# One decode-attention kernel, two attention blocks: each TensorE round takes its own group's PV, V of the last two groups in two parts, and wo of A with four heads side by side

## The chip, the cores and the metric

The kernel runs on one core of a Trainium2 chip. A core has five engines with instruction streams of their own: TensorE (PE in the profile, its weight loads PEld), VectorE (DVE), ScalarE (ACT), GpSimd (POOL) and SyncE (SP). Sixteen DMA engines move data from the chip's memory into the core's own memory (SBUF); TensorE writes its results into PSUM. The streams meet only at semaphores. The metric is the device time of one execution in microseconds; the kernel before has a median of 672.45 us over 3 runs (671.89 to 672.48).

## The reference

There are two independent attention blocks, A and B, of the same sizes. Each decodes one token: one query row, 32 heads of 128 numbers, and a cache of 8192 keys and values per head, all in bf16.

```python
# for A and for B; x: 1x512, k_cache and v_cache: 32 heads x 8192 x 128
q = x @ wq                                  # 512 x 4096, then 32 heads of 128
scores = einsum("hd,hkd->hk", q, k_cache) * 128 ** -0.5
p = softmax(scores)                         # over 8192 keys
o = einsum("hk,hkd->hd", p, v_cache)
y = o.reshape(1, 4096) @ wo                 # 4096 x 512
# the result is y of A and y of B side by side: 1 x 1024
```

Each cache is 64 MiB, and there are four of them. Each of the four weight matrices is 4 MiB.

## The kernel before

**Tiling.** Four heads make a group; there are N = 16 groups, eight of A and then eight of B. A group's K is 8 MiB: the 128 partitions hold 4 heads times 32 stretches of 256 keys, so that a partition has 256 keys (T) of 128 numbers. There are two K buffers (`kn`, used in turn) and one V buffer (`vn`). The query weights of A and B (`wq`) lie in the V buffer at the start, and the output weights (`wo`) in K buffer 0 at the end.

**One group.** VectorE multiplies K in place by the query in four quarters (`plan_mul`, L307). TensorE sums each quarter over the 128 numbers of a key in 16 matmuls against the identity into one of two PSUM halves (`scores`, L461), and VectorE adds up what is left (`plan_sr`, L312). The largest score of each head is found by VectorE and two small TensorE transposes (`plan_max`, L319 to L323, with L499 and L502 on TensorE). ScalarE then takes four exponentials, one per head, and their row sums (`plan_exp`, L335). For PV, TensorE makes one matmul of four columns for each of the 256 key positions, with a tile of V as the weights (L490), after one matmul that adds up the row sums (L483). VectorE divides by the sums (`plan_o`, L341 and L342).

**The order of TensorE's work** is written out in `pe_program`. A hardware loop of 17 rounds makes, in round r, the first three quarters of group r's scores, then PV of group r-1, then the fourth quarter of group r's scores and its maximum. The last round has no scores. In it stands, ahead of PV of group 15, a block (`prog[mid0:mid1]`) that moves the finished heads into another layout (`relayout`, L388 to L394), multiplies A's heads by A's wo (`mm_a`, L405: 32 matmuls of one output row, 512 columns each) and the first 16 heads of B by their part of B's wo (`mm_b`, L419). What is left of B's wo follows the loop.

**VectorE's order** for group n is: two quarters of the product, `plan_o` of group n-2, then products and sums in turn, and the maximum.

**The DMA queue.** All bulk loads are issued by SyncE in one order, each after the wait that frees its buffer:

```python
load_v(n, pv_done(n - 1) if n else q_done)   # V of group n: PV of group n-1 has read the buffer
load_k(n + 2)                                # K of group n+2: scores of group n are done
```

So the order in the queue is wq of A and B, K0, K1, V0, K2, V1, K3 and so on. After V14 come wo of A, the first part of B's wo (16 heads), V15 in two parts (192 and 64 of the 256 key positions, `VT = 192`, the second with a semaphore of its own, `s_v2`), and then the other parts of B's wo in shrinking pieces.

Of the kernel before, what the change touches and what calls it, by code (L numbers as in the profile page):

```python
# [8 lines left out]
BF16 = mybir.dt.bfloat16  # L9
F32 = mybir.dt.float32  # L10

P = 128
# [11 lines left out]
class _Plan:  # L24
# [6 lines left out]
    def wait(self, eng, mark):  # L31
        if mark is None:
            return
        ctr, val = mark
        if val <= 0 or self.waited.get((eng, ctr.name), 0) >= val:
            return
        self.waited[(eng, ctr.name)] = val
        self.prog[eng].append((None, ctr, val))

    def op(self, eng, fn, ctr=None, needs=(), inc=1):  # L40
        for m in needs:
            self.wait(eng, m)
        self.prog[eng].append((fn, ctr, inc))
        if ctr is None:
            return None
        ctr.n += inc
        return ctr, ctr.n
# [28 lines left out]
def bass_concat_heads__mha_block_cached__gqa_block_cached__decode_kernel(  # L76
# [19 lines left out]
    H, Sk, Dh = ks[0].shape[1:]  # L96
    D = xs[0].shape[2]
    NOUT = wos[0].shape[1]
# [4 lines left out]
    G = 4  # L103
    HP = P // G
    T = Sk // HP
    assert T == 256
    GA = H // G
    N = NA * GA
    NB = 4
    HT = T // NB  # L110
    DW = 512 // HT
    VT = 192
# [7 lines left out]
    with ExitStack() as st:  # L120
# [3 lines left out]
        def sb(name, shape, dt):  # L124
            return ec(nc.sbuf_tensor(name, shape, dt))

        kn = [sb("k%d" % i, [P, T, Dh], BF16) for i in range(2)]
        vn = sb("vn", [P, T, Dh], BF16)
# [5 lines left out]
        wo_buf = [kflat[0][:, a * H * NOUT:(a + 1) * H * NOUT] for a in range(NA)]  # L134
        wo_sb = [b.rearrange("p (j n) -> p j n", n=NOUT) for b in wo_buf]

        qbc = sb("qbc", [P, N, Dh], BF16)
        pt = sb("pt", [P, T, G], BF16)
        s_sb = sb("s_sb", [P, T], F32)
        xrow = sb("xrow", [1, NA, D], BF16)  # L140
        xb = sb("xb", [P, NA, C, HP], BF16)
        ones_bf = sb("ones_bf", [P, P], BF16)
        ones_f = sb("ones_f", [P, P], F32)
        ident = sb("ident", [P, P], BF16)
        ident_f = sb("ident_f", [P, P], F32)
        m1 = sb("m1", [P, 1], F32)
        gm = sb("gm", [1, G], F32)
        gmx = sb("gmx", [1, P], F32)
        negb = sb("negb", [P, N], F32)
        rsum = sb("rsum", [P, G], F32)  # L150
# [3 lines left out]
        o2 = sb("o2", [P, NA, H], BF16)  # L154
# [3 lines left out]
        out_a = sb("out_a", [1, NOUT], BF16)  # L158
# [6 lines left out]
        acc = ps("acc", [P, 512])  # L165
        mtp = ps("mtp", [P, 512])
        bmp = ps("bmp", [P, 512])
        misc = ps("misc", [P, 512])
        yps = [ps("yps%d" % i, [P, 512]) for i in range(2)]

        pl = _Plan()
        op, wait = pl.op, pl.wait
# [22 lines left out]
        def pv_done(n):  # L195
            return c_pv, n + 1
# [7 lines left out]
        def dma(eng, dst, src, c, needs=()):  # L204
            return op(eng, lambda e: e.dma_start(dst, src), c, needs, inc=16)  # L205


        def const(fn, needs=()):
            return op("POOL", fn, c_pool, needs)

        i_onesb = const(lambda e: e.memset(ones_bf[:], 1.0))
        i_onesf = const(lambda e: e.memset(ones_f[:], 1.0))
        i_ident = const(lambda e: e.affine_select(
            out=ident[:], in_=ones_bf[:], pattern=[[1, P]], compare_op=ALU.is_equal,
            fill=0.0, base=0, channel_multiplier=-1), [i_onesb])
# [18 lines left out]
        def load_v(n, need, t0=0, t1=T, c=None):  # L234
            a, i = divmod(n, GA)
            src = vs[a][0, G * i:G * (i + 1)].rearrange("h (p t) d -> (h p) (t d)", p=HP)
            v_in[n] = dma("SP", vflat[:, t0 * Dh:t1 * Dh], src[:, t0 * Dh:t1 * Dh], c or s_v, [need])
# [30 lines left out]
        q_done = None  # L268
# [36 lines left out]
        def plan_mul(n, h):  # L305
            k = kn[n % 2][:, h * HT:(h + 1) * HT, :]
            mul_done[n, h] = op("DVE", lambda e: e.tensor_tensor(  # L307
                k, k, qbc[:, n:n + 1, :].broadcast_to([P, HT, Dh]), ALU.mult),
                c_mul, [k_in[n], qbc_ready[n]])

        def plan_sr(n, h):
            sr_done[n, h] = op("DVE", lambda e: e.tensor_reduce(  # L312
                s_sb[:, h * HT:(h + 1) * HT],
                rps[:, h % 2, :].rearrange("p (t d) -> p t d", d=DW), AX.X, ALU.add),
                c_sr, [red_done(n, h), p_done.get(n - 1)])
# [23 lines left out]
        def plan_o(n):  # L339
            a, i = divmod(n, GA)  # L340
            m = op("DVE", lambda e: e.reciprocal(rinv[:, n, :], misc[:, 0:G]), c_dve, [sum_done(n)])  # L341
            o_done[n] = op("DVE", lambda e: e.tensor_tensor(  # L342
                oD[:, a, G * i:G * (i + 1)], acc[:, 0:G], rinv[:, n, :], ALU.mult),
                c_o, [pv_done(n), m])

        load_k(0)
        load_k(1)
        for n in range(N):
            if n < N - 1:
                load_v(n, pv_done(n - 1) if n else q_done)  # L350
                if n + 2 < N:
                    load_k(n + 2)
            plan_mul(n, 0)
            plan_mul(n, 1)
            if n >= 2:
                plan_o(n - 2)
            plan_sr(n, 0)
            plan_mul(n, 2)
            plan_sr(n, 1)
            plan_mul(n, 3)  # L360
            plan_sr(n, 2)
            plan_sr(n, 3)
            plan_max(n)
            plan_exp(n)

# [5 lines left out]
        load_v(N - 1, None, VT, T, s_v2)  # L371
        for g in range(NPRE, len(WOB)):
            load_wob(g)

        plan_o(N - 2)


        mid0 = len(pl.prog["PE"])
# [19 lines left out]
        for h0, n, rows in WOB:  # L398
            if rows:
                relayout(1, h0, n)  # L400

        def mm_a(e):
            r = None
            for j in range(H):
                r = e.matmul(yps[0][0:1, :], o2[:, 0, j:j + 1], wo_sb[0][:, j, :],  # L405
                             start=(j == 0), stop=(j == H - 1))
            return r
        m = op("PE", mm_a, c_pe, [o2_ready[0, 0], woa_in, y_free[0]])
        m = op("ACT", lambda e: e.copy(out_a[:], yps[0][0:1, :]), c_act, [m])
        done_a = dma("ACT", out[0][:, 0:NOUT], out_a[:], s_out[0], [m])  # L410

        def mm_b(g):
            h0, n, rows = WOB[g]
# [11 lines left out]

        for g in range(NPRE):
            mm_b(g)
        wait("PE", misc_free[0])
        mid1 = len(pl.prog["PE"])


# [13 lines left out]
        def pe_program(e):  # L445
            prog = pl.prog["PE"]
            _emit(e, prog[:mid0])
            w_mul = _Stepped(e, c_mul, 1, 1)
            w_sr = _Stepped(e, c_sr, SR0 - 1, 1)
            w_g = _Stepped(e, c_g, 1, 1)  # L450
            w_o = _Stepped(e, c_o, O0, 1)
            w_p = _Stepped(e, c_p, G, G)
            w_v = _Stepped(e, s_v, 16, 16)

            def scores(slot, hs):
                for h in hs:
                    w_mul.wait()
                    w_sr.wait()
                    r = None
                    for i in range(Dh // DW):  # L460
                        r = e.matmul(  # L461
                            rps[:, h % 2, :].rearrange("p (t d) -> p t d", d=DW), ident[:],
                            kn[slot][:, h * HT:(h + 1) * HT, i * DW:(i + 1) * DW],
                            start=(i == 0), stop=(i == Dh // DW - 1))
                    r.then_inc(c_red.sem, 1)
                    w_mul.grow()
                    w_sr.grow()

            def scores_of(r, hs):
                with e.If(r % 2 == 0):  # L470
                    scores(0, hs)
                with e.Else():
                    scores(1, hs)

            with e.Fori(0, N + 1) as r:
                with e.If(r < N):
                    scores_of(r, range(0, NB - 1))
                with e.If(r == N):
                    _emit(e, prog[mid0:mid1])
                with e.If(r > 0):  # L480
                    w_o.wait()
                    w_p.wait()
                    e.matmul(misc[:, 0:G], ones_f[:], rsum[:], start=True, stop=True).then_inc(c_sum.sem, 1)  # L483
                    w_v.wait()
                    m = None
                    for t in range(T):
                        if t == VT:
                            with e.If(r == N):
                                e.wait_ge(s_v2.sem, 16)
                        m = e.matmul(acc[:, 0:G], vn[:, t, :], pt[:, t, :],  # L490
                                     start=(t == 0), stop=(t == T - 1))
                    m.then_inc(c_pv.sem, 1)
                    w_o.grow()
                    w_p.grow()
                    w_v.grow()
                with e.If(r < N):
                    scores_of(r, range(NB - 1, NB))
                    w_g.wait()
                    e.matmul(mtp[0:1, 0:P], m1[:], ident_f[:], start=True, stop=True).then_inc(c_gx.sem, 1)  # L499
                    w_g.grow()  # L500
                    w_g.wait()
                    e.matmul(bmp[:, 0:1], gmx[:], ones_f[0:1, 0:1], start=True, stop=True).then_inc(c_bc.sem, 1)  # L502
                    w_g.grow()
            _emit(e, prog[mid1:])

        for name, at in (("SP", block.sync), ("PE", block.tensor), ("ACT", block.scalar),
# [35 lines left out]
```

## Time and profile before

| | |
|---|---|
| median of 3 runs | 672.45 us (671.89 to 672.48) |
| the profiled execution: its time, its span | 671.92 us, 670.2 us |
| bytes read from memory | 285.21 MB |
| PE matmul busy | 439.5 us, 66% |
| VectorE busy | 342.6 us, 51% |
| ScalarE busy | 62.2 us, 9% |
| mean granted TensorE clock | 0.757 |

Everything below refers to the profiled execution, with times in microseconds from the start of its span. The page of the profile gives each engine's busy time, and the span in 40 slices with the busy share of the DMA engines and what they moved. A view of stretches gives the same for any piece of the span: after its limits and length come the busy time of PE, PEld, VectorE, ScalarE and GpSimd (with the number of instructions in brackets), the granted TensorE clock, the busy share of the DMA engines, and GB/s. A DMA packet is counted in the stretch in which it starts. The timeline has a line for each run of alike instructions: start, length, engine, line, operation, what it writes and reads, how many, and in brackets how long the engine was idle before it and what ended that. The list of DMA issues gives the time from issue to landing.

### The profile page before, as it was taken

The numbers are of one execution on the slowest core, as the hardware profiler recorded it, in microseconds if no ns is written. First come the engines' busy times: TensorE is split into PE (matmuls) and PEld (weight loads), VectorE is DVE, ScalarE is ACT, GpSimd is POOL, SyncE is SP. The second block draws the span as 40 slices with busy tenths as digits, with TensorE's granted clock in tenths as the row PEclk, the third lists the DMA queues.
The fourth block names the chain that finished last, engine by engine and source line by source line (L and its number), as shares of the span: only waits on it lengthen the run. The fifth ranks groups of instructions, "written<-read, shape, count | busy, mean of one in ns | idle before, by whom it ended". The sixth has DMA issues, their size and how long they took to land.

```text
span 670.2 us, 11845 instructions
## 1 busy us (share of the span) xinstructions
PE 439.5 (66%) x5453; PEld 241.9 (36%) x5453; DVE 342.6 (51%) x229; ACT 62.2 (9%) x151; POOL 2.0 (0%) x10
## 2 busy tenths in 40 slices
PE   2225696969577584948759483865938387694877
PEld 1002252525235261513426161442616144261626
DVE  1046565657292735629183663909266380836520
ACT  1100202020200102020100202020020201002020
POOL 1000000000000000000000000000000000000000
PEclk9659797979777676978776697877658796676886
DMA  9999999999999999999999999999999999999996
GB/s 376 438 438 429 435 391 375 438 438 439 438 434 438 434 426 396 438 438 438 438 438 438 438 438 438 430 438 430 426 411 430 438 438 434 438 438 438 406 448 278
DMA packets 6198, 285.33 MB, mean 426 GB/s; under 512 B 683, under 2 KB 1198, under 8 KB 1326
## 3 DMA queue, kind: packets, MB, share of 16 engines
q1 hardware_dynamic: 6184, 285.22, 98.7%
q8 instruction: 5, 0.08, 0.1%
q14 instruction: 3, 0.02, 0.0%
q10 hardware_dynamic: 6, 0.00, 0.0%
HBM read 285.21 MB, written 0.00 MB: 426 GB/s over the span
## 4 chain that ended last, share of the span: by engine, by line
DMA 60%; PE 27%; DVE 11%; issue 1%; SPq 0%
DMA vn<-in_B_v_cache_dram 19%; PE rps L461 15%; DMA k<-in_B_k_cache_dram 14%; DMA k<-in_A_k_cache_dram 13%; PE acc L490 12%; DVE k L307 10%; DMA vn<-in_A_v_cache_dram 9%; DMA k<-in_B_wo_dram 4%; DVE s_sb L312 1%; SPq L205 0%; DVE m L319 0%; PE mtp L499 0%; DVE gm L320 0%; PE misc L483 0%; DVE gmx L323 0%
## 5 line engine op out<-in xcount | busy, mean ns | idle before, releaser
L461 PE MATMUL rps<-k,ident 128*128 128x512 bf16 x1024 | 296.2, 458 | 171.0 <-DVE k L307 163.3
L307 DVE TENSOR_TENSOR k<-k,qbc 128x8192 bf16<-128x8192 bf16 x64 | 281.4, 4418 | 94.7 <-DMA k<-in_A_k_cache_dram 57.0
L461 PEld LDWEIGHTS rps<-k,ident 128*128 128x128 bf16 x1024 | 112.5, 114 | 342.8 <-DVE k L307 173.3
L312 DVE TENSOR_REDUCE s_sb<-rps 128x64 f32<-128x512 f32 x64 | 44.1, 689 | 196.2 <-PE rps L461 196.2
L490 PE MATMUL acc<-pt,vn 128*128 128x4 bf16 x4096 | 108.9, 165 | 6.1 <-DMA vn<-in_B_v_cache_dram 3.8
L490 PEld LDWEIGHTS acc<-pt,vn 128*128 128x128 bf16 x4096 | 108.2, 100 | 7.0 <-DMA vn<-in_B_v_cache_dram 4.3
L335 ACT ACTIVATE pt<-s_sb,negb 32x256 bf16<-32x256 f32 x64 | 54.8, 856 | 1.9
L328 ACT ACTIVATE negb<-bmp 128x1 f32<-128x1 f32 x16 | 2.7, 171 | 560.1 <-PE bmp L502 560.1
L499 PE MATMUL mtp<-ident_f,m 128*1 128x128 f32 x32 | 6.1, 271 | 19.8 <-DVE m L319 19.8
L335 ACT ACTIVATION_READ_ACCUMULATOR pt<-s_sb,negb 32x1 f32 x64 | 15.9, 248 | 0.0
L277 PE MATMUL yps<-vn,xb 128*32 128x512 bf16 x64 | 7.3, 630 | 10.6 <-DMA vn<-in_B_wq_dram 6.0
L502 PE MATMUL bmp<-ones_f,gmx 1*128 1x1 f32 x32 | 6.2, 259 | 9.9 <-DVE gmx L323 9.9
L499 PEld LDWEIGHTS mtp<-ident_f,m 128*1 128x1 f32 x32 | 1.4, 81 | 27.7 <-DVE m L319 27.7
L502 PEld LDWEIGHTS bmp<-ones_f,gmx 1*128 1x128 f32 x32 | 4.8, 186 | 14.6 <-DVE gmx L323 14.6
L405 PE MATMUL yps<-k,o 128*1 128x512 bf16 x32 | 8.4, 429 | 0.0
L320 DVE TENSOR_REDUCE gm<-mtp 1x4 f32<-1x128 f32 x16 | 4.4, 278 | 7.5 <-PE mtp L499 7.5
L341 DVE RECIPROCAL rinv<-misc 128x4 f32<-128x4 f32 x16 | 2.8, 174 | 10.1 <-PE misc L483 10.1
L277 PEld LDWEIGHTS yps<-vn,xb 128*32 128x32 bf16 x64 | 2.7, 134 | 14.3 <-issue 7.5
L342 DVE TENSOR_TENSOR oD<-acc,rinv 128x4 bf16<-128x4 f32 x16 | 2.6, 163 | 9.7 <-PE acc L490 8.1
L319 DVE TENSOR_REDUCE m<-s_sb 128x1 f32<-128x256 f32 x16 | 6.7, 420 | 0.5
L483 PEld LDWEIGHTS misc<-rsum,ones_f 128*128 128x128 f32 x32 | 6.0, 190 | 2.2
L260 PE MATMUL misc<-ones_bf,xrow 1*128 1x32 bf16 x8 | 0.4, 192 | 8.0 <-DMA xrow<-in_B_x_dram 8.0
(35 smaller groups left out, 32.5 us busy)
## 6 DMA issues: line engine op xcount, KB each, us to landing
vn<-in_B_v_cache_dram SPq DMA_DIRECT2D x1, 6144.0 KB, 22.3
vn<-in_A_wq_dram SPq DMA_DIRECT2D x1, 4096.0 KB, 12.2
vn<-in_B_wq_dram SPq DMA_DIRECT2D x1, 4096.0 KB, 21.4
k<-in_A_wo_dram SPq DMA_DIRECT2D x1, 4096.0 KB, 35.8
k<-in_B_wo_dram SPq DMA_DIRECT2D x1, 2048.0 KB, 40.3
vn<-in_B_v_cache_dram SPq DMA_DIRECT2D x1, 2048.0 KB, 26.8
k<-in_B_wo_dram SPq DMA_DIRECT2D x1, 1024.0 KB, 28.8
k<-in_B_wo_dram SPq DMA_DIRECT2D x1, 512.0 KB, 29.6
```

The costliest lines, as they stand in the source:

```text
L277: r = e.matmul(yps[j % 2][hh * HP:(hh + 1) * HP, :].rearrange("p (i d) -> p i d", d=Dh), xb[:, a, c, :], w, start=(c == 0), stop=(c == C - 1))
L307: mul_done[n, h] = op("DVE", lambda e: e.tensor_tensor(k, k, qbc[:, n:n + 1, :].broadcast_to([P, HT, Dh]), ALU.mult), c_mul, [k_in[n], qbc ...
L312: sr_done[n, h] = op("DVE", lambda e: e.tensor_reduce(s_sb[:, h * HT:(h + 1) * HT], rps[:, h % 2, :].rearrange("p (t d) -> p t d", d=DW), ...
L319: op("DVE", lambda e: e.tensor_reduce(m1[:], s_sb[:], AX.X, ALU.max), c_g)
L320: m = op("DVE", lambda e: e.tensor_reduce(gm[:], mtp[0:1, 0:P].rearrange("o (h p) -> o h p", h=G), AX.X, ALU.max), c_dve, [gx_done(n)])
L335: p_done[n] = op("ACT", lambda e, h=h, q=q: e.activation(pt[q, :, h], s_sb[q, :], AF.Exp, bias=negb[q, n:n + 1], scale=scale, accum_out=rs ...
L405: r = e.matmul(yps[0][0:1, :], o2[:, 0, j:j + 1], wo_sb[0][:, j, :], start=(j == 0), stop=(j == H - 1))
L461: r = e.matmul(rps[:, h % 2, :].rearrange("p (t d) -> p t d", d=DW), ident[:], kn[slot][:, h * HT:(h + 1) * HT, i * DW:(i + 1) * DW], star ...
L483: e.matmul(misc[:, 0:G], ones_f[:], rsum[:], start=True, stop=True).then_inc(c_sum.sem, 1)
L490: m = e.matmul(acc[:, 0:G], vn[:, t, :], pt[:, t, :], start=(t == 0), stop=(t == T - 1))
L499: e.matmul(mtp[0:1, 0:P], m1[:], ident_f[:], start=True, stop=True).then_inc(c_gx.sem, 1)
L502: e.matmul(bmp[:, 0:1], gmx[:], ones_f[0:1, 0:1], start=True, stop=True).then_inc(c_bc.sem, 1)
```

## The change

- TensorE's loop has 16 rounds. Round r makes all four quarters of group r's scores, its maximum, and then PV of the same group r. The block with the output weights stands in the last round between the maximum of group 15 and PV of group 15.
- VectorE's order for group n becomes: four quarters of the product, `plan_o` of group n-1, four sums, the maximum.
- V of group 14 is loaded in two parts as well (192 and 64 key positions), and the second semaphore is waited for in the last two rounds, with a growing value.
- A's product with wo puts head j at the output rows 32*(j mod 4) to 32*(j mod 4)+31, with its one column repeated 32 times as weights, so that four heads add up in four strips of PSUM. VectorE copies the 128x512 result to SBUF (`ya_sb`, in the memory of the queries, after the last product has read them), and one more matmul with a column of 1/32 (`part`) adds the 128 rows into one. Then ScalarE's copy and the store follow as before.
- A column of 1/32 is written by GpSimd at the start.

```diff
-        qbc = sb("qbc", [P, N, Dh], BF16)
+        qmem = sb("qmem", [P, N * Dh // 2], F32)
+        qbc = qmem[:].bitcast(BF16).rearrange("p (n d) -> p n d", d=Dh)
+        ya_sb = qmem[:, 0:NOUT]
...
+        part = sb("part", [P, 1], F32)
...
+        const(lambda e: e.memset(part[:], 1.0 / HP))
...
+            if n < N - 2:
+                load_v(n, pv_done(n - 1) if n else q_done)
+            elif n == N - 2:
+                load_v(n, pv_done(n - 1), 0, VT)
+                load_v(n, None, VT, T, s_v2)
             if n < N - 1:
-                load_v(n, pv_done(n - 1) if n else q_done)
                 if n + 2 < N:
                     load_k(n + 2)
-            plan_mul(n, 0)
-            plan_mul(n, 1)
-            if n >= 2:
-                plan_o(n - 2)
-            plan_sr(n, 0)
-            plan_mul(n, 2)
-            plan_sr(n, 1)
-            plan_mul(n, 3)
-            plan_sr(n, 2)
-            plan_sr(n, 3)
+            for h in range(NB):
+                plan_mul(n, h)
+            if n:
+                plan_o(n - 1)
+            for h in range(NB):
+                plan_sr(n, h)
             plan_max(n)
             plan_exp(n)
...
-
-        plan_o(N - 2)
...
             for j in range(H):
-                r = e.matmul(yps[0][0:1, :], o2[:, 0, j:j + 1], wo_sb[0][:, j, :],
-                             start=(j == 0), stop=(j == H - 1))
+                k = j % G * HP
+                r = e.matmul(yps[0][k:k + HP, :], o2[:, 0, j:j + 1].broadcast_to([P, HP]),
+                             wo_sb[0][:, j, :], start=(j < G), stop=(j >= H - G))
             return r
         m = op("PE", mm_a, c_pe, [o2_ready[0, 0], woa_in, y_free[0]])
-        m = op("ACT", lambda e: e.copy(out_a[:], yps[0][0:1, :]), c_act, [m])
-        done_a = dma("ACT", out[0][:, 0:NOUT], out_a[:], s_out[0], [m])
+        ya_ready = op("DVE", lambda e: e.tensor_copy(ya_sb, yps[0][:]), c_dve, [m, mul_done[N - 1, NB - 1]])
...
-        wait("PE", misc_free[0])
+        m = op("PE", lambda e: e.matmul(mtp[0:1, :], part[:], ya_sb, start=True, stop=True),
+               c_pe, [ya_ready, misc_free[0]])
+        m = op("ACT", lambda e: e.copy(out_a[:], mtp[0:1, :]), c_act, [m])
+        done_a = dma("ACT", out[0][:, 0:NOUT], out_a[:], s_out[0], [m])
...
-            with e.Fori(0, N + 1) as r:
-                with e.If(r < N):
-                    scores_of(r, range(0, NB - 1))
-                with e.If(r == N):
+            with e.Fori(0, N) as r:
+                with e.If(r % 2 == 0):
+                    scores(0, range(NB))
+                with e.Else():
+                    scores(1, range(NB))
+                w_g.wait()
+                e.matmul(mtp[0:1, 0:P], m1[:], ident_f[:], start=True, stop=True).then_inc(c_gx.sem, 1)
+                w_g.grow()
+                w_g.wait()
+                e.matmul(bmp[:, 0:1], gmx[:], ones_f[0:1, 0:1], start=True, stop=True).then_inc(c_bc.sem, 1)
+                w_g.grow()
+                with e.If(r == N - 1):
                     _emit(e, prog[mid0:mid1])
-                with e.If(r > 0):
-                    w_o.wait()
...
+                w_o.wait()
+                w_p.wait()
+                e.matmul(misc[:, 0:G], ones_f[:], rsum[:], start=True, stop=True).then_inc(c_sum.sem, 1)
+                w_v.wait()
+                m = None
+                for t in range(T):
+                    if t == VT:
+                        with e.If(r >= N - 2):
+                            w_v2.wait()
+                            w_v2.grow()
+                    m = e.matmul(acc[:, 0:G], vn[:, t, :], pt[:, t, :],
+                                 start=(t == 0), stop=(t == T - 1))
+                m.then_inc(c_pv.sem, 1)
+                w_o.grow()
+                w_p.grow()
+                w_v.grow()
             _emit(e, prog[mid1:])
```

More of the change, by code (lines that the diff above doesn't have):

```diff
@@ L453, in pe_program @@
             w_v = _Stepped(e, s_v, 16, 16)
+            w_v2 = _Stepped(e, s_v2, 16, 16)
             def scores(slot, hs):
@@ L473, in scores_of @@
                     scores(1, hs)
-            with e.Fori(0, N + 1) as r:
-                with e.If(r < N):
-                    scores_of(r, range(0, NB - 1))
-                with e.If(r == N):
-                    _emit(e, prog[mid0:mid1])
-                with e.If(r > 0):
-                    w_o.wait()
[L482 to L503, printed above, removed]
```

## The prediction

> **What bounds the kernel now.** I read the page's DMA rows first, then the chain that ended last, then the stretches around the weak slices, and last the timeline of the end.
>
> ```profile
> DMA  9999999999999999999999999999999999999996
> GB/s 376 438 438 429 435 391 375 438 438 439 438 434 438 434 426 396 438 438 438 438 438 438 438 438 438 430 438 430 426 411 430 438 438 434 438 438 438 406 448 278
> ...
> DMA 60%; PE 27%; DVE 11%; issue 1%; SPq 0%
> ```
>
> The DMA engines are busy in all slices but the last, and DMA leads the chain. The slices to look at are the sixth and seventh (84 to 117 us) and the end. The stretches (length, busy times, granted clock, DMA share, GB/s):
>
> ```profile
> 95.00:97.00 2.00, 2.00 (x85) 2.00 (x83) 1.76 (x2) 0.00 (x0) 0.00 (x0) 1.00 0.68 295
> 97.00:98.00 1.00, 1.00 (x46) 1.00 (x44) 0.00 (x0) 0.00 (x0) 0.00 (x0) 1.00 1.21 524
> 98.00:99.00 1.00, 1.00 (x46) 1.00 (x43) 0.00 (x0) 0.00 (x0) 0.00 (x0) 0.97 0.30 131
> 99.00:100.00 1.00, 1.00 (x44) 1.00 (x41) 0.00 (x0) 0.00 (x0) 0.00 (x0) 0.50 0.16 66
> 100.00:101.00 1.00, 1.00 (x43) 1.00 (x41) 0.00 (x0) 0.00 (x0) 0.00 (x0) 0.50 0.15 66
> 101.00:102.00 1.00, 0.88 (x25) 0.67 (x23) 0.00 (x0) 0.00 (x0) 0.00 (x0) 0.50 0.00 0
> 102.00:103.00 1.00, 1.00 (x4) 0.31 (x3) 0.00 (x0) 0.00 (x0) 0.00 (x0) 0.50 2.36 786
> 103.00:104.00 1.00, 1.00 (x4) 0.43 (x3) 0.00 (x0) 0.00 (x0) 0.00 (x0) 0.50 0.69 262
> 106.00:628.00 522.00, 354.90 (x4299) 194.65 (x4296) 294.56 (x181) 50.45 (x126) 0.00 (x0) 0.76 1.00 433
> ```
>
> From 106 to 628 us the engines carry 433 GB/s at a share of 1.00: no reordering of compute can gain anything there. Before it the queue runs dry once. From 95 to 104 us it moves 2 x 295 + 524 + 131 + 66 + 66 + 0 + 786 + 262 = 2425 KB where 433 GB/s would give 3897: 1472 KB, or 3.4 us. The cause is in the issue rows of SyncE and the landings:
>
> ```profile
> 26.41 0.33 SPq L205 DMA_DIRECT2D vn<-in_A_v_cache_dram  x1
> 73.35 0.33 SPq L205 DMA_DIRECT2D k<-in_A_k_cache_dram  x1
> 101.66 0.33 SPq L205 DMA_DIRECT2D vn<-in_A_v_cache_dram  x1
> ...
> vn<-in_A_v_cache_dram SPq DMA_DIRECT2D x1, 57.3
> ...
> k<-in_A_k_cache_dram SPq DMA_DIRECT2D x1, 29.7
> vn<-in_A_v_cache_dram SPq DMA_DIRECT2D x1, 22.0
> ```
>
> V0 is issued at 26.41 and lands at 83.7, K2 lands at 73.35 + 29.7 = 103.0, and V1 is issued only at 101.66, because it waits for PV of group 0, which in the old order stands behind three quarters of group 1's scores.
>
> **Part 1, the round with its own PV: removes the dry spot.** The rows for its terms:
>
> ```profile
> L307 DVE TENSOR_TENSOR k<-k,qbc 128x8192 bf16<-128x8192 bf16 x64 | 281.4, 4418 | 94.7 <-DMA k<-in_A_k_cache_dram 57.0
> ...
> L312 DVE TENSOR_REDUCE s_sb<-rps 128x64 f32<-128x512 f32 x64 | 44.1, 689 | 196.2 <-PE rps L461 196.2
> ...
> 42.02 8.76 DVE L307 TENSOR_TENSOR k<-k,qbc 128x8192 bf16<-128x8192 bf16 x2 [38.61 <-DMA k<-in_A_k_cache_dram]
> ...
> 574.70 9.79 PE L461 MATMUL rps<-k,ident 128*128 128x512 bf16 x32 [8.00 <-DVE k L307]
> ...
> 586.15 3.63 PE L461 MATMUL rps<-k,ident 128*128 128x512 bf16 x16 [1.66 <-DVE k L307]
> ```
>
> Group 0: the products run from 42.0 to 59.7 (4 x 4.42), the first sum ends at 60.4, and the last two quarters of scores take 7.3 (2 x 3.63) to 9.8 us: K2 is issued at 68 to 70 instead of 73.35. Maximum and exponentials take 6.3 us (640.35 to 646.7 for group 15: start of the last sum below, to the last exponential), so they end before V0 lands. PV of group 0 runs from 83.7 to 90.5 (6.74 us), and V1 is issued 11 us earlier than now, 9 us before the bulk of K2 is through (the packets that begin at 97 end near 99.5, at 433/16 GB/s for 65.5 KB). The dry spot goes.
>
> What that gives is not 3.4 us for every engine. A landing counts the latest engine, and the rows after 98 us show four late ones (131 is two packets, 66 is one): two begin their last packet about 1.4 us behind the bulk, two about 3 us. For the latest of them V1's landing comes 123.66 - 103.05 = 20.6 us after K2's, where a transfer takes 19.35 in the steady part (below): only 1.25 us lost. The dry spot is also where the other engines waited for the late ones; without it, the lateness is carried to the end. Where it comes from:
>
> ```profile
> 63.02 4.84 issue
> ...
> q8 instruction: 3, 0.05, 1.9%
> ```
>
> These are the chain of the first round and the queues from 60 to 75 us: TensorE stands 4.84 us at its jump over the still unused PV block, while instruction loads (16 KB each) go through the same DMA engines. In the new order round 0 doesn't jump over PV, so I expect these loads one at a time. I take the smaller lateness, 1.4 us less than now: 1.25 + 1.4 = 2.65, say 2.6 us. Ends for the range: 1.25 (lateness as now) and 3.4 (none).
>
> The Trainium skill says of this ("DMA: Bandwidth & Descriptors", Queues, rings and completion order) that each DMA engine takes the queue rows it has work for in turn, a packet at a time; by that rule an instruction load delays just the engine it falls on, and what is lost is the worst engine's, so the gain would be 1.25 us wherever two loads meet on an engine. The late packets agree; that a load is the cause no row here proves.
>
> **Part 2, the steady rounds: nothing, and what hides it.** Let V of group n-1 land at 0.
>
> ```profile
> 169.80 31.79 DMA vn<-in_A_v_cache_dram
> ...
> 285.94 31.75 DMA vn<-in_A_v_cache_dram
> ...
> 596.51 31.73 DMA vn<-in_B_v_cache_dram
> ```
>
> Landings at 201.59 and 317.69 are three rounds apart: 38.70 each, 19.35 per transfer. PV ends at 6.8 and V(n) is issued as now, 31.8 - 19.35 = 12.4 us ahead of its turn. The four quarters of scores, now in one piece, take 9.8 + 2 x 3.46 = 16.7 (3.63 less the 0.17 of a last drain) and end at 23.5, which releases K(n+2), now after PV and one quarter. It is due when V(n) lands at 38.7: 15 us of cover. The exponentials end at 23.5 + 6.3 = 29.8, 9 us before V(n) is there. VectorE has 4 x 4.42 + 4 x 0.69 + 1.3 = 21.7 us of work in 38.7; the next products start at 25.7 and end at 43.4, ahead of the next scores' need of a sum. Were every quarter as slow as a first one (9.8 - 3.46 = 6.3), the exponentials would end at 38.3: still hidden. So no queue runs dry, at a cost of 0.
>
> **Part 3, the end.** Here the cover is thin. Rows:
>
> ```profile
> vn<-in_B_v_cache_dram SPq DMA_DIRECT2D x1, 6144.0 KB, 22.3
> ...
> 635.12 0.80 SPq L205 DMA_DIRECT2D vn<-in_B_v_cache_dram  x2
> ...
> 640.35 0.69 DVE L312 TENSOR_REDUCE s_sb<-rps 128x64 f32<-128x512 f32 x1 [10.59 <-PE rps L461]
> ...
> 641.55 0.38 PE L499 MATMUL mtp<-ident_f,m 128*1 128x128 f32 x2 [1.24 <-DVE m L319]
> ...
> 642.88 0.29 DVE L388 TENSOR_TENSOR zb<-oD,mask 128x128 bf16<-128x128 bf16 x1
> ...
> 645.70 8.43 PE L405 MATMUL yps<-k,o 128*1 128x512 bf16 x32
> ...
> 654.06 1.75 PE L419 MATMUL yps<-o,k 128*128 128x1 bf16 x64
> ...
> 655.72 0.36 PE L483 MATMUL misc<-rsum,ones_f 128*128 128x4 f32 x2
> ...
> 657.43 6.97 PE L490 MATMUL acc<-pt,vn 128*128 128x4 bf16 x256 [1.36 <-DMA vn<-in_B_v_cache_dram]
> ...
> 666.88 0.82 PE L419 MATMUL yps<-oD,k 128*128 128x1 bf16 x16 [0.18 <-DMA k<-in_B_wo_dram]
> ...
> 646.43 0.25 ACT L335 ACTIVATION_READ_ACCUMULATOR pt<-s_sb,negb 32x1 f32 x1
> ...
> 22.68 3.64 PE L277 MATMUL yps<-vn,xb 128*32 128x512 bf16 x32 [5.95 <-DMA vn<-in_B_wq_dram]
> ```
>
> Now V15's first part lands at 635.12 + 22.3 = 657.4, PV of group 15 starts on it, and the last matmuls end at 667.70, each held by a landing of wo. In the new order, before any gain of part 1 (all of it shifts with V14's landing at 628.24):
> - V14's first part lands a quarter of 19.35 = 4.84 earlier, so PV of group 14 ends 6.97 - 4.84 = 2.1 after the whole: 630.4. V15 is issued then, ahead of its turn. Only now do group 15's scores start, where three quarters were done before: 630.4 + 16.7 = 647.1.
> - Sum, maximum, transposes: 642.88 - 640.35 = 2.5, less 0.45 for `plan_o` gone from there; relayout 645.70 - 642.88 = 2.8. Wo of A starts at 652.0.
> - Its 32 matmuls cost 8.43 in one strip. The nearest row for four strips is q's projection, 32 matmuls of the same columns in four strips: 3.64. I take that; bounds 2.0 (the same overlap at the full clock; L277's row ran at half) and 8.43 (no overlap). 655.6.
> - 64 matmuls with B's wo, 1.7: 657.3. VectorE's copy of 128x512 (0.69, as the sums) lies beside them.
> - The added matmul with `part`: four times the columns of the 0.38 pair, 1.5 (bounds 0.9, if 0.17 of the pair is drain, and 1.9 at half clock): 658.8. GpSimd's extra memset lies at the start beside the loads.
> - Row sums 0.15, PV 6.9 (its second part is there at 662.3), the last 64 matmuls 1.75: 667.6.
>
> That is 0.1 us inside 667.70. With an uncertainty of a microsecond either way, the cost is 0 to 1; I take 0.3. Ends: 0 and 4.7 (no overlap of the strips).
>
> The Trainium skill ("TensorE: Matmul & The Clock Gate", Measured speedup vs the span model) gives 2.38x for three column strips, not 3x. Four at that rate take 4 / 3.17 of the time of full overlap; if 3.64 were full overlap, that makes 4.6 us, an estimate, an end at 668.6 and a sum 0.6 us worse. The 3.64 was measured in this kernel with four strips, and it decides.
>
> **Sum.** 671.92 - 2.6 + 0.3 = 669.6 against the profiled execution. This lies 0.5 below the median of 672.45, so a median would be 669.6 to 670.1; I forecast 670.0.
>
> **Rivals.**
> - *The lateness stays as now.* Gain 1.25 - 0.3: 671.4. For it: the number of instruction loads can hardly change, and one load alone would do by the rule cited above. Against: the two that met did so at a jump that goes. Chance 0.20.
> - *PV of group 0 runs on code that must still be loaded* and waits twice 4.84 us: it ends at 100, V1 comes when K2 is through, and the dry spot stays: 672.4. Against it: TensorE waits for V0 long before, with time to load. Chance 0.07.
> - *Slower: the four strips don't overlap.* Then wo of A holds back PV of group 15, and the end comes 4.7 us behind 667.70: 672.45 - 2.6 + 4.7 = 674.6. It decides from a `mm_a` of 6.3 us up, where it has used up the 2.6 of part 1. Against it stands the projection's row; for it, that its weights are one column repeated. Chance 0.09. Other losses (code that no longer stays in the loop, a load late in a steady round): 0.06, near 676.
> - *The forecast itself*, 668.4 to 671.1: chance 0.58.
>
> **Numbers.** 0.2% is 1.34 us, about what a measurement of this kernel can tell from no change. The forecast's range lies wholly on the faster side; the two rivals in between are the same; the last two slower. With edges blurred by 0.5 us: faster 0.59, same 0.25, slower 0.16. The range 668.2 to 672.8 leaves out the slow cases and a little below.
>
> **What would show it.** No stretch near 100 us below 400 GB/s; V1 issued near 90 us; V14 landing 1.2 to 3.4 us before 628.2; L405 with 32 matmuls in 2 to 4 us; PV of group 15 starting within 1 us of its landing. Wrong if the rate drops in a steady round, if PV of group 15 starts late, or if one engine's lateness eats the gain.

## The result and the profile after

The changed kernel takes 668.01 us (median of 4 runs, 667.88 to 668.09) against 672.2 us before (now also of 4 runs, 671.89 to 672.48): a ratio of 0.9938, 95% interval 0.992 to 0.9955. The profiled execution took 668.09 us with a span of 666.4 us, where it had been 671.92 and 670.2. The forecast was 670.0 with a range of 668.2 to 672.8: the direction was right, the gain is 4.2 us where 2.45 was forecast, and the time lies 0.2 us below the range.

The page of the changed kernel, slices and head of the chain:

```profile
DMA  9999999999999999999999999999999999999996
GB/s 378 441 441 438 438 435 437 417 421 441 433 433 441 437 441 429 425 425 441 433 433 437 437 441 433 417 433 441 433 429 441 437 441 429 421 433 426 420 458 271
...
DMA 77%; PE 17%; DVE 3%; another core or an unknown queue 1%; issue 1%; ACT 1%; SPq 1%
```

The two slices of 391 and 375 GB/s near 100 us are gone (435 and 437 now). VectorE and TensorE, 38% of the chain before, are 20% now. The same stretches around 100 us as in the prediction (length, busy times, clock, DMA share, GB/s), in the changed kernel:

```profile
98.00:99.00 1.00, 1.00 (x6) 0.45 (x5) 0.64 (x1) 0.00 (x0) 0.00 (x0) 1.00 0.60 262
99.00:100.00 1.00, 1.00 (x6) 0.49 (x5) 0.00 (x0) 0.00 (x0) 0.00 (x0) 1.00 1.82 786
100.00:101.00 1.00, 1.00 (x7) 0.41 (x6) 0.00 (x0) 0.00 (x0) 0.00 (x0) 1.00 0.30 131
101.00:102.00 1.00, 1.00 (x6) 0.47 (x5) 0.60 (x1) 0.00 (x0) 0.00 (x0) 1.00 1.66 721
...
106.00:624.00 518.00, 325.02 (x4420) 194.78 (x4419) 290.83 (x176) 50.61 (x126) 0.00 (x0) 0.71 1.00 433
```

Between 99 and 102 us the queue moves 786, 131 and 721 GB/s, where it moved 66, 66 and 0. The steady rate is the same 433. The first rounds in the chain of waits of the changed kernel, and how long V0 and V1 took from issue (26.61 and 92.53) to landing:

```profile
60.40 9.41 PE rps L468 x32
...
75.31 0.87 ACT pt L339 x2
...
82.30 4.24 PE acc L505 x153
86.54 3.05 issue
89.59 2.92 PE acc L505 x103
92.51 0.02 issue
92.53 28.45 DMA vn<-in_A_v_cache_dram
```

```profile
vn<-in_A_v_cache_dram SPq DMA_DIRECT2D x1, 55.7
...
vn<-in_A_v_cache_dram SPq DMA_DIRECT2D x1, 28.4
```

Group 0's exponentials end at 76.2, V0 lands at 82.26, PV of group 0 stands 3.05 us in its middle ("issue": it waits for nothing that the profile shows; a load of 16 KB of instructions starts at 87.18 us, so I take it to wait for that), and V1 is issued at 92.53 and lands at 120.98 (123.62 before). And the end:

```profile
619.58 6.98 PE L505 MATMUL acc<-pt,vn 128*128 128x4 bf16 x256 [3.34 <-DMA vn<-in_B_v_cache_dram]
626.86 16.38 PE L468 MATMUL rps<-k,ident 128*128 128x512 bf16 x64 [0.29 <-issue]
...
647.85 2.71 PE L409 MATMUL yps<-k,o 128*32 128x512 bf16 x32
650.50 1.86 PE L422 MATMUL yps<-o,k 128*128 128x1 bf16 x64
652.29 1.87 PE L431 MATMUL mtp<-qmem,part 128*1 128x512 f32 x2
654.09 0.59 PE L497 MATMUL misc<-rsum,ones_f 128*128 128x4 f32 x2
654.53 6.97 PE L505 MATMUL acc<-pt,vn 128*128 128x4 bf16 x256
661.36 1.49 PE L422 MATMUL yps<-o,k 128*128 128x1 bf16 x48
663.04 0.84 PE L422 MATMUL yps<-oD,k 128*128 128x1 bf16 x16 [0.18 <-DMA k<-in_B_wo_dram]
```

This is the timeline of TensorE. V14's second part lands at 624.43 (628.24 before), and the last 16 matmuls still wait for the last piece of wo. From V14's landing to the end of the last matmul it is 39.45 us, before 39.46: the end costs nothing, and the 3.8 us that the span lost are all in V14's landing.

### The profile page after: what moved, and what is told of

Read it like the earlier page. It is cut to its first block, busy times and chain, and to the rows that moved or that the text cites. A ratio compares the mean times of both kernels' runs of the same rounds, so it can differ in the third digit from the quotient of the medians.

```text
span 666.4 us, 11727 instructions
## 1 busy us (share of the span) xinstructions
PE 409.6 (61%) x5455; PEld 240.8 (36%) x5455; DVE 344.9 (52%) x230; ACT 62.4 (9%) x151; POOL 2.1 (0%) x11
## 4 chain that ended last, share of the span: by engine, by line
DMA 77%; PE 17%; DVE 3%; another core or an unknown queue 1%; issue 1%; ACT 1%; SPq 1%
DMA vn<-in_A_v_cache_dram 33%; DMA vn<-in_B_v_cache_dram 33%; PE acc L505 16%; DMA k<-in_A_k_cache_dram 6%; DMA k<-in_B_wo_dram 5%; DVE k L311 3%; PE rps L468 1%; ACT pt L339 1%; SPq L208 1%; DVE s_sb L316 0%; PE misc L497 0%; DVE m L323 0%; PE mtp L488 0%; PE bmp L491 0%
## 5 line engine op out<-in xcount | busy, mean ns | idle before, releaser
L311 DVE TENSOR_TENSOR k<-k,qmem 128x8192 bf16<-128x8192 bf16 x64 | 278.6, 4406 | 38.8 <-DMA k<-in_A_k_cache_dram 38.8
L468 PE MATMUL rps<-k,ident 128*128 128x512 bf16 x1024 | 259.2, 420 | 28.1 <-DVE k L311 20.2
L505 PE MATMUL acc<-pt,vn 128*128 128x4 bf16 x4096 | 111.9, 166 | 117.7 <-DMA vn<-in_A_v_cache_dram 61.6
L468 PEld LDWEIGHTS rps<-k,ident 128*128 128x128 bf16 x1024 | 107.5, 106 | 174.0 <-issue 51.6
L505 PEld LDWEIGHTS acc<-pt,vn 128*128 128x128 bf16 x4096 | 110.7, 104 | 119.0 <-DMA vn<-in_A_v_cache_dram 62.3
L497 PE MATMUL misc<-rsum,ones_f 128*128 128x4 f32 x32 | 9.0, 351 | 58.7 <-ACT pt L339 58.7
L497 PEld LDWEIGHTS misc<-rsum,ones_f 128*128 128x128 f32 x32 | 8.0, 311 | 61.3 <-issue 61.3
```

The lines of the kernel that those rows point to most:

```text
L311: mul_done[n, h] = op("DVE", lambda e: e.tensor_tensor(k, k, qbc[:, n:n + 1, :].broadcast_to([P, HT, Dh]), ALU.mult), c_mul, [k_in[n], qbc ...
L468: r = e.matmul(rps[:, h % 2, :].rearrange("p (t d) -> p t d", d=DW), ident[:], kn[slot][:, h * HT:(h + 1) * HT, i * DW:(i + 1) * DW], star ...
L505: m = e.matmul(acc[:, 0:G], vn[:, t, :], pt[:, t, :], start=(t == 0), stop=(t == T - 1))
```

## The experiments

The table sums up the landings of all kernels: each is the issue plus the time from issue to landing, in us of the profiled execution. From V1 to V14 there are 26 transfers of 8 MiB, 503.1 us at 19.35 each. In the last two kernels the dry spot lies inside that stretch.

| kernel | dry spot | V0 lands | V1 lands | V1 to V14 | V14 lands | median us |
|---|---|---|---|---|---|---|
| before | V1 | 83.74 | 123.62 | 504.62 | 628.24 | 672.2 |
| e4, strips alone | V1 | 83.64 | 123.97 | 505.09 | 629.06 | 671.70 |
| e5, V1 held back | V1 | 82.13 | 123.54 | 504.54 | 628.08 | 672.29 |
| after | none | 82.26 | 120.98 | 503.45 | 624.43 | 668.01 |
| e7, unused block | none | 82.10 | 121.02 | 503.40 | 624.42 | 668.19 |
| e1, one strip | none | 82.20 | 120.90 | 503.34 | 624.24 | 670.49 |
| e2, V14 whole | none | 82.07 | 120.83 | 503.49 | 624.32 | 672.25 |
| e3, round alone | none | 82.15 | 120.86 | 504.02 | 624.88 | 675.43 |
| e6, old round, PV earlier | none | 83.92 | 122.62 | 503.16 | 625.78 | 675.96 (one run) |
| e8, V10 held back | V10 | 82.21 | 120.91 | 506.94 | 627.85 | 671.69 |
| e9, V12 held back | V12 | 82.15 | 120.87 | 506.80 | 627.67 | 671.28 |

Four kernels take the change apart.

**e1: wo of A in one strip again.** The two blocks of the diff around `mm_a` and `part` are undone, all else as changed:

```diff
-                r = e.matmul(yps[0][k:k + HP, :], o2[:, 0, j:j + 1].broadcast_to([P, HP]),
-                             wo_sb[0][:, j, :], start=(j < G), stop=(j >= H - G))
+                r = e.matmul(yps[0][0:1, :], o2[:, 0, j:j + 1], wo_sb[0][:, j, :],
+                             start=(j == 0), stop=(j == H - 1))
```

> The changed kernel with wo of A in one strip again (32 matmuls of one output row, no added matmul). Theory 1 (the strips keep TensorE's chain just inside the last landings): the 32 matmuls take 8.4 us instead of 2.71, the added matmul of 1.87 goes, so PV of group 15 starts 3.9 us later than its 654.53; with some 0.2 us of cover the time is 668.0 + 3.7 = 671.7. Theory 2 (the end hangs on DMA with room to spare, as before the change): 668.0.

Measured: 670.49 us; against before a ratio of 0.9992 (0.998 to 1.0003). So the strips are worth about 2.5 of the 4.2 us. TensorE's timeline of e1:

```profile
647.26 8.75 PE L408 MATMUL yps<-k,o 128*1 128x512 bf16 x32
655.95 1.75 PE L422 MATMUL yps<-o,k 128*128 128x1 bf16 x64
657.57 0.36 PE L494 MATMUL misc<-rsum,ones_f 128*128 128x4 f32 x2
657.79 6.76 PE L502 MATMUL acc<-pt,vn 128*128 128x4 bf16 x256
664.41 1.42 PE L422 MATMUL yps<-o,k 128*128 128x1 bf16 x48
665.69 0.56 PE L422 MATMUL yps<-oD,k 128*128 128x1 bf16 x16
```

PV of group 15 starts at 657.79 instead of 654.53, and no matmul after it waits for a landing any more: TensorE's own chain is the end. It comes 2.4 us later (666.25 against 663.88), less than the 3.9 I had worked out, because the changed kernel's last matmuls had been waiting for wo, and e1's chain reached this point 0.6 us sooner.

**e2: V of group 14 whole.**

```diff
-            elif n == N - 2:
-                load_v(n, pv_done(n - 1), 0, VT)
-                load_v(n, None, VT, T, s_v2)
-                        with e.If(r >= N - 2):
+                        with e.If(r >= N - 1):
```

(The first branch now covers group 14 too.)

> The changed kernel with V of group 14 loaded in one piece. Theory 1 (group 15's scores stand behind PV of group 14 and the chain has no room): PV of group 14 ends 4.8 us later, everything behind it too, less 0.2 us of cover: 668.0 + 4.6 = 672.6. Theory 2 (room to spare): 668.0.

Measured: 672.25 us, ratio to before 1.0008 (0.9998 to 1.0017). V14 lands at 624.32, no later than in the changed kernel, and PV of group 15 starts 4.8 us later, at 659.33. Splitting V14 is worth the whole gain: the new round delays group 15's scores behind PV of group 14, and the split takes that back.

**e3: the round alone**, with both edits of e1 and e2.

> The new round alone, with V of group 14 whole and wo of A in one strip. Theory 1: both delays add, 4.8 + 3.9 - 0.2 = 8.5, so 676.5: slower than the kernel before by 4 us. Theory 2 (the round alone gives the whole gain): 668.0. Landings up to V13 as in the changed kernel under both.

Measured: 675.43 us, ratio 1.0065 (1.0044 to 1.0086): slower than before although V14 lands 3.4 us sooner. PV of group 15 starts at 662.71.

**e4: the strips alone**, put into the kernel before.

> The kernel before with wo of A in four strips and the added matmul, nothing else. Theory 1 (there the end waits for landings): PV of group 15 still starts at 657.4 on its landing, 672.2, no change. Theory 2 (the strips have a gain of their own): 670 or less.

Measured: 671.70 us beside 671.78 for before in the same session, ratio 0.9999 (0.9986 to 1.0012). TensorE's timeline of e4 shows the 32 matmuls, and the 5.66 us that TensorE then waits for V15:

```profile
646.40 3.24 PE L410 MATMUL yps<-k,o 128*32 128x512 bf16 x32
649.58 1.75 PE L423 MATMUL yps<-o,k 128*128 128x1 bf16 x64
651.26 1.02 PE L432 MATMUL mtp<-qmem,part 128*1 128x512 f32 x2
652.21 0.39 PE L490 MATMUL misc<-rsum,ones_f 128*128 128x4 f32 x2
658.25 6.99 PE L497 MATMUL acc<-pt,vn 128*128 128x4 bf16 x256 [5.66 <-DMA vn<-in_B_v_cache_dram]
```

So the strips have no gain of their own; they pay only where the round has moved work to the end.

The other five ask where the landings' 3.8 us came from.

**e5: V1 held back in the changed kernel**, so that the dry spot returns and nothing else does:

```diff
             if n < N - 2:
+                if n == 1:
+                    wait("SP", red_done(1, 1))
                 load_v(n, pv_done(n - 1) if n else q_done)
```

> The changed kernel, but V of group 1 is issued only when the second quarter of group 1's scores is done (about 101.6 us, as in the kernel before). Theory 1 (the gain is the dry spot at 100 us; a landing counts the latest engine, and what is lost there is lost to the end): V1 lands at about 123.4 instead of 120.98; the engines are in step afterwards, so that later instruction loads show in a landing (0.3 to 1.3 us more in all): 670.6 to 671.7. Theory 2 (the gain comes from the rounds or the end, not from this spot): at most 668.5.

Measured: 672.29 us, ratio to before 1.0013 (1.0002 to 1.0024): the gain is gone, and 0.6 us more than the top of what I expected. V1 is issued at 101.63; the stretches and the landing:

```profile
99.00:100.00 1.00, 1.00 (x7) 0.47 (x5) 0.00 (x0) 0.00 (x0) 0.00 (x0) 1.00 0.01 0
100.00:101.00 1.00, 1.00 (x6) 0.41 (x5) 0.00 (x0) 0.00 (x0) 0.00 (x0) 1.00 0.00 0
101.00:102.00 1.00, 1.00 (x6) 0.49 (x5) 0.36 (x1) 0.00 (x0) 0.00 (x0) 1.00 0.00 0
```

```profile
vn<-in_A_v_cache_dram SPq DMA_DIRECT2D x1, 21.9
```

V1 lands 2.56 us later than in the changed kernel, and V14 3.65 us later. The other 1.1 us are lost in two later transfers, 19.70 and 20.33 us long where the changed kernel has 19.36 and 19.60; an instruction load of 8 KB falls in each of them in both kernels (near 173 and 483 us).

**e6: the old round with PV after the first quarter of the scores.** The dry spot goes in another way; the jump over the unused PV block stays.

```diff
-                    scores_of(r, range(0, NB - 1))
+                    scores_of(r, range(0, 1))
...
-                    scores_of(r, range(NB - 1, NB))
+                    scores_of(r, range(1, NB))
```

> The kernel before, with PV of the last group behind the first quarter of a group's scores instead of the third. V1 is issued at about 93, the dry spot goes, the jump over the unused PV block in round 0 stays. Theory 1 (lateness of single DMA engines is carried on where the queue doesn't run dry): V0 lands at 83.7 as before, V1 at 122.4 (1.25 earlier than before), and V14 at 626 to 627 instead of 628.24. Theory 2 (all engines gain the dry time): V1 lands at 120.2 or earlier, V14 at 624.8 or earlier. The end is another matter: three quarters of group 15's scores come behind PV of group 14, so the time is some 675 under both.

Measured: V0 at 83.92, V1 at 122.62, V14 at 625.78, 675.96 us in one run. V1 was issued at 97.79, not 93. The first theory fits V0 and V1: they stay late as before, and V1 gains 1.0, not 3.4. But V14 gains 2.5, because from V1 to V14 nothing at all is lost (503.16). Beside the changed kernel, V1 lands 1.6 us later and V14 1.35: lateness is carried on. The queues and the issue of K1 in e6, around the jump, show something of use:

```profile
q8 instruction: 2, 0.03, 58.8%
```

```profile
k<-in_A_k_cache_dram SPq DMA_DIRECT2D x1, 62.1
```

Here two loads of instructions meet at 51 us, and K1, just in transfer, takes 62.1 from issue to landing instead of 60.7 with one load at that time in the kernel before and in the changed one. In those with two loads at 63 us (before, e4) it is V0 that takes 20.9 instead of 19.3 us. Two loads that meet cost about 1.4 to 1.5 us more than one.

**e7: an unused block of 128 matmuls in the changed kernel's loop.**

```diff
+                with e.If(r == N):
+                    for t in range(128):
+                        e.matmul(acc[:, 0:G], vn[:, t, :], pt[:, t, :], start=True, stop=True)
                 with e.If(r == N - 1):
                     _emit(e, prog[mid0:mid1])
```

> The changed kernel with a block of 128 matmuls in the loop that no round enters, between the maximum and the block with the output weights, so that round 0 jumps over 30 KB more of instructions. Theory 1 (two instruction loads that meet on the DMA engines at a jump make the latest engine later): V0 lands at 83.6 instead of 82.26, and that stays: 669.2. Theory 2 (instruction loads don't matter to landings): 668.0 and V0 at 82.3. Theory 3 (the loop no longer stays loaded): instruction loads in every round and 670 or more.

Measured: 668.19 us, ratio to before 0.9947 (0.9928 to 0.9966). It doesn't test the first theory, since the loads never met: four come one by one between 77 and 100 us. Nor do further loads come in the rounds, so the third theory is out. The queues of e7 in that time, and V1:

```profile
q8 instruction: 4, 0.07, 1.1%
...
vn<-in_A_v_cache_dram SPq DMA_DIRECT2D x1, 23.6
```

It shows something else: V1 is issued 4.9 us later here, at 97.44, and lands as in the changed kernel, at 121.02. Of the 9 us of cover that the prediction gave V1, counted from an issue at 90.5, the 6.9 up to this issue are shown.

**e8 and e9: the dry spot moved.** The wait of e5 with `red_done(10, 2)` ahead of V10, and with `red_done(12, 2)` ahead of V12.

> The changed kernel, but V of group 10 is issued only when the third quarter of group 10's scores is done (about 449.7 us), when K of group 11 is all but landed. Theory 1 (a dry spot costs its own 2.4 us, issue to landing 21.9 instead of 19.35, and puts the DMA engines in step again, so that the instruction load near 482 us, which costs 0.25 us in the changed kernel, then shows in full): V10 lands at 471.6 instead of 469.29, K12 takes about 20.3 us instead of 19.60, V14 lands near 627.5, 671.1. Theory 2 (a dry spot costs no more than itself): K12 takes 19.6, V14 lands near 626.8, 670.4. Loads before it as in the changed kernel under both.

> The same for V of group 12, issued at about 527.8, behind the last load of instructions before the end. Both theories: K12 takes 19.6, V12 lands at 549.7 instead of 546.95, nothing is lost after it, V14 lands near 627.2, 670.8. If a late dry spot cost nothing because the engines make it up, V14 would land at 624.4 and the time be 668.0.

Measured: e8 671.69 us (ratio to before 0.9996, 0.9985 to 1.0007), e9 671.28 us (0.9988, 0.9979 to 0.9998). The issue rows of V10 in e8 and of V12 in e9:

```profile
vn<-in_B_v_cache_dram SPq DMA_DIRECT2D x1, 22.0
```

```profile
vn<-in_B_v_cache_dram SPq DMA_DIRECT2D x1, 22.1
```

V10 lands at 472.23, 2.9 us later than in the changed kernel, and V12 at 550.22, 3.3 later. With e5 this gives one price: a transfer of 19.35 us takes 21.9 to 22.1 when it finds the queue empty, 2.6 to 2.7 us on top of the time by which its issue comes after the landing before it (0.15, 0.4 and 0.5 us in the three). By the same price V1 before, issued 1.4 us ahead of K2's landing, should lose 1.2, and its transfer takes 20.55, 1.2 more than 19.35; in e4, issued 0.9 us ahead, it should lose 1.7 and loses 1.65. The theory that a dry spot makes the next instruction load show in full falls with e8: K12's transfer, with the load at 483 us in it, takes 19.68 us, not 20.3 (the next section shows why). e8 loses another 0.4 us in V13 and the K after it, in which no load falls; the cause of that is open.

## Why the prediction was right or wrong

- **The dry spot and its removal: right.** K2 is issued at 69.82 (forecast 68 to 70), the exponentials end at 76.2, V0's landing isn't missed, and e5 shows by itself that a late V1 takes the whole gain back. V1 is issued at 92.53 rather than 90.5, since PV of group 0 stood once for 3.05 us, the second rival in small; e7 shows that this was covered.
- **What it gives at V1's landing: right.** I took 1.25 for the dry spot and 1.4 for the lateness from two instruction loads, 2.65. Measured: V0 lands 1.48 sooner, V1 2.64. In the changed kernel the loads come one at a time (three between 76 and 96 us, and no landing in that time is late), so the rival by which the lateness stays fell.
- **The steady rounds "nothing": the step that failed.** No queue runs dry there, in that the step was right, and each issue keeps its cover. But of 106 to 628 us I said that no reordering of compute can gain anything, because the rate is 433 GB/s at a share of 1.00 and three rounds in a row take 38.70 each, and so I took what is gained at V1's landing for the whole gain. The three rounds hold neither of the two transfers of the kernel before that were longer than 19.35: V2 with 19.92 and K12 with 20.34, now 19.35 and 19.60. That is 1.3 us, of which 1.2 are left from V1 to V14 (504.62 and 503.45 in the table). Their issue rows of before (V2 at 135.72, K12 at 445.76) had been there to read:

```profile
vn<-in_A_v_cache_dram SPq DMA_DIRECT2D x1, 27.1
...
k<-in_B_k_cache_dram SPq DMA_DIRECT2D x1, 47.1
```

  K12's 47.1 stands out among the 44.8 to 46.0 of the other K in full rounds. For the same reason the upper bound of 3.4 us was none: it was what the dry spot costs in bytes at that place, a mean over the DMA engines, and a dry spot at V1 costs 3.65 in e5 by the time V14 lands.
- **Why the later losses went.** Landings alone leave it open: the transfer that holds the load near 157 to 173 us loses 0.35 to 1.0 us in the three kernels with the dry spot at V1 and nothing in the other eight, but the one with the load near 480 to 500 us loses 1.0 in those three, 0 to 0.4 in seven of the others, and 0.9 in e3.

  The traces also keep the time of each of the 16 rises of a transfer's semaphore, of which the landing is the last. In a steady transfer without a load, all 16 come 19.35 us after those of the transfer before (but for the two of e8 named above). In these 22 transfers with a load (two in each of the 11 kernels) fifteen still do, to within 0.04 us, and one comes 0.94 to 1.06 us later. A third load, near 261 to 273 us, makes one rise about 0.7 us later and shows in no landing. I read this as a load that delays one of the 16 DMA engines. The Trainium skill ("DMA: Bandwidth & Descriptors", Why a DMA increments its semaphore by 16 and not by 1) says that a DMA runs on up to 16 engines that finish independently, and that the semaphore counts them. The traces agree: they show 16 rises, and one that moves alone.

  What a landing loses is the part of the delay that goes beyond the lead that this rise had on the last one (us):

  | transfer | lead before | delay | lost at the landing |
  |---|---|---|---|
  | before, V2 | 0.45 | 1.01 | 0.57 |
  | before, K12 | 0.08 | 1.06 | 0.99 |
  | after, K4 | 1.71 | 0.97 | 0.01 |
  | after, K12 | 0.72 | 0.97 | 0.25 |
  | e3, K12 | 0.06 | 0.97 | 0.91 |
  | e6, V11 | 1.98 | 0.96 | 0.01 |
  | e8, K12 | 0.64 | 0.98 | 0.33 |

  So the dry spot also takes away the leads that hide later loads. Behind it the 16 rises lie within 0.6 to 1.0 us in the five kernels that have one (0.8 at V1 in the kernel before); in the changed kernel they spread over 2.0 at V1, twelve of them 1.4 or more ahead of the last. The mean of the 16 comes 3.5 us sooner there than before, which is about the 3.4 that I had counted in bytes, but the last only 2.64. The rest comes at V2 and K12, where the kernel before loses 1.6 us to its loads, and the changed kernel 0.3 to the same two loads at K4 and K12. I had written that lateness is carried to the end, and didn't see that it hides the delays that follow. Part of it is luck: e3 lands within 0.15 us of the changed kernel up to V10, but at K12 its load meets a rise with no lead and costs 0.7 us more.
- **The end: right in kind, slightly too dear.** I took 0.3 us, and it cost nothing. The terms: PV of group 14 ended 2.1 us after V14's landing, as forecast; scores 16.38 (16.7); wo of A 2.71 (3.64); the added matmul 1.87 (1.5, bound 1.9 at the half clock; the granted clock was 0.50). The cover was as thin as said: PV of group 15 starts 1.0 us after its landing, and e1 and e2 show what it costs without either part.
- **The slower rival, no overlap of the strips:** wrong about the strips, but its mechanism is e1. It ended at 670.49, not 674.6, mostly because V14's landing gave 1.2 us more and because I set the added matmul on top of the 8.43, where one strip doesn't need it.
- **From the sum to a median.** The sum said 669.6 and I moved it to 670.0 for the 0.5 us between the profiled execution and the median. The terms in order: 2.64 at V1, 1.2 in the later transfers, 0 at the end make 3.8; the profiled executions differ by 671.92 - 668.09 = 3.8.

## What to carry to other kernels

Where the DMA engines are busy to the end, look for the places where the queue runs dry, and price one by the transfer's time from issue to landing against its neighbours, not by the bytes missing at that place; then list every single transfer's time, because a mean rate hides the odd one that is a microsecond longer. Look also at how far the 16 rises of its semaphore lie apart: here a delay of one showed in a landing only as far as it exceeded its lead on the last. A reordering that feeds the queue sooner moves work to the end: here the round alone lost more than 3 us, and two small parts made it a gain of 4 (wo in four strips, which has no gain of its own in e4, and V14 in two parts, which was not run alone).

## What the runs showed of the hardware that was not expected

- A transfer of 8 MiB that finds the queue empty takes 21.9 to 22.1 us from issue to landing; in a full queue it lands 19.35 after the transfer before it (e5, e8, e9).
- Loads of instructions of 16 KB, which come where TensorE enters new code, lengthen a bulk transfer: K1 takes 20.3 to 20.9 us with one load in it, and 22.15 in e6 with two that meet. One load delays one of the 16 rises of the semaphore by 1.53 to 1.58 us (K1 in ten kernels), a load of 8 KB by 0.94 to 1.06 us in 22 transfers and by about 0.7 in the 11 others; in a landing only what exceeds the lead of that rise shows.
- Four output strips made the 32 matmuls of wo 2.6 times as fast at the same place (8.43 to 3.24 us, before and e4), 3.1 times in the changed kernel (2.71). The Trainium skill ("TensorE: Matmul & The Clock Gate", Measured speedup vs the span model) has 2.38 for three strips; the granted clock was 0.83, 0.58 and 0.68 in the three rows, so they don't give a sharper number.
